# Two attention decodes in one kernel: five rows of B's output weights loaded in sixteen small pieces, to a tile of their own

## The chip, the cores and the metric

The kernel runs on one core of one Trainium2 chip. The metric is the device time of one execution in microseconds (us). Before the change the median of three runs is 255.6 us (255.55 to 255.86).

## The reference, cut to what matters

The program computes two independent attention steps, A and B, for one query position each, and puts their outputs side by side. Each has 32 query heads and 16 key/value heads of 128 elements (two query heads share one key/value head), a model width of 576, and a cache of 8192 positions. A looks only at the last 2048 of them, B at all.

```
q = (x @ wq)                       # 576 -> 32 heads x 128
scores = q . k * 128 ** -0.5       # A: last 2048 positions, B: all 8192
o = softmax(scores) . v
out = o.reshape(1, 32 * 128) @ wo  # 4096 -> 576, for A and for B
return concatenate([a, b], axis=-1)
```

All inputs are bf16. The caches that are read are the bulk: 2 MB of K and 2 MB of V for each of B's 16 heads, 512 KB each for A's. `wq` and `wo` have 4.7 MB for each problem.

## The kernel before, in words

**Instructions and their waits.** The kernel is written as five lists of instructions, one for each engine's queue. `op` (L41) puts a compute instruction on a list, `load` (L47) a DMA. Each names the instructions or loads that it needs; `emit` (L53) turns these names into waits on semaphores, in the order of the list, so an instruction that waits holds up what stands behind it on its queue. A load adds 16 to its semaphore when it has landed.

**The ring.** Nearly all that is loaded goes through one large buffer, `ring` (L112), 86 x 1024 bf16 elements in each of 128 partitions. `place` (L165) gives a load the next stretch of it, starting over at the end, and makes the load wait for the last users of whatever stood there before. It also cycles through 24 semaphores. All loads of weights and caches are issued by SyncE (the queue named SPq), one after the other: first A's and B's `wq`, then the units, then `wo`.

**Units and slabs.** A unit is the K or the V of one head of one problem (L195 to L199): 64 units, 32 of 2 MB for B and 32 of 512 KB for A, of which the V units come some units behind their K. Partition p holds a run of consecutive positions of the cache, so each load has an outer dimension of 128 partitions and one long run in each (16 KB for B, 4 KB for A). A unit is worked on in slabs of 2048 positions, four for B and one for A, so 80 slabs for K and 80 for V. `units` is walked at L457, where `place` is called for each (L464).

**Work on a slab.** TensorE transposes the 16 tiles of a K slab (`st_T`, L310), ScalarE and VectorE copy them out (L328, L331), TensorE multiplies with the query (`st_S`, L342). When the five slabs of a head are done, a shared maximum, the exponential and a transpose of the probabilities follow, and nine slabs behind K, TensorE multiplies them with V (`st_V`, L426). The heads' outputs are turned and collected in `oT` (L453).

**The end.** After the last head the sums are divided out, and `oP` (L527) holds the outputs as 32 columns for each problem: partition p of column k stands for row 32 * p + k of the output weights. So `wo` is loaded with 32 of its rows in each partition (1152 bytes a row), in the pieces that `NWO` lists (L28): two of 16 rows for A, and 8, 8, 6, 4, 3, 2 and 1 for B (L471 to L478). The rows of a piece are consecutive in each partition. For each piece, TensorE runs two matmuls a row (one for each half of the 576 columns), each 1 x 288 wide, accumulated over the 32 rows (L533 to L543, named F0.c for A and F1.c for B). A piece's matmuls wait for that piece alone. Behind A's two pieces and behind B's last piece, ScalarE and VectorE each copy out one half (L547, L550), and SyncE stores the result (L551), a load in reverse with an outer dimension of 2.

Of the kernel before, what the change touches and what calls it, by code (L numbers as in the profile page):

```python
# [4 lines left out]
BF16 = mybir.dt.bfloat16  # L5
# [6 lines left out]
HQ = 32  # L12
G = 16
DH = 128
DM = 576
# [4 lines left out]
SLAB = 2048  # L20
NI = SK // SLAB + 1
IA = NI - 1
RING = 86 * 1024
NSEM = 24
NKT = 3
LAG = 9
QP = 32 * NI
NWO = [[16, 16], [8, 8, 6, 4, 3, 2, 1]]  # L28


class Prog:
# [9 lines left out]
    def op(self, eng, fn, deps=(), name=None):  # L41
        self.ops[eng].append((fn, tuple(deps), name, None))
        if name is not None:
            assert name not in self.where, name
            self.where[name] = (eng, len(self.ops[eng]) - 1)

    def load(self, eng, fn, sem, value, deps=(), name=None):  # L47
        self.ops[eng].append((fn, tuple(deps), None, sem))
        if name is not None:
            assert name not in self.dma, name  # L50
            self.dma[name] = (sem, value)
# [54 lines left out]
def bass_concat_heads__sliding_block_cached__gqa_block_cached__decode_kernel(nc, A_x, A_k_cache, A_v_cache, A_wq, A_wo,  # L106
                         B_x, B_k_cache, B_v_cache, B_wq, B_wo, out):
    xs, ks, vs = [A_x, B_x], [A_k_cache, B_k_cache], [A_v_cache, B_v_cache]
    wqs, wos = [A_wq, B_wq], [A_wo, B_wo]


    ring = nc.alloc_sbuf_tensor("ring", [128, RING], BF16)  # L112
    ktb = nc.alloc_sbuf_tensor("ktb", [128, NKT, SLAB], BF16)
# [23 lines left out]
    oq = nc.alloc_sbuf_tensor("oq", [128, 2, HQ], BF16)  # L137
    oP = nc.alloc_sbuf_tensor("oP", [128, 2, HQ], BF16)
    warm = nc.alloc_sbuf_tensor("warm", [128, 8], F32)
    outsb = nc.alloc_sbuf_tensor("outsb", [128, 288], BF16)  # L140

    tb = [nc.alloc_psum_tensor("tb%d" % b, [128, 512], F32) for b in range(3)]
# [13 lines left out]
    op, load = pg.op, pg.load  # L156
    s_x = nc.alloc_semaphore("s_x")
    s_ld = [nc.alloc_semaphore("s_ld%d" % i) for i in range(NSEM)]
    s_out = nc.alloc_semaphore("s_out")


# [3 lines left out]
    def place(size, uses, issue, name):  # L165
        if at[0] + size > RING:
            at[0] = 0
        lo, hi = at[0], at[0] + size
        at[0] = hi
        deps = []  # L170
        for r in list(live):
            if r[0] < hi and lo < r[1]:
                deps += r[2]
                live.remove(r)
        n = nload[0]
        nload[0] += 1
        if n >= NSEM:
            deps += uses_of[n - NSEM]
        uses_of.append(list(uses))
        live.append((lo, hi, list(uses)))  # L180
        t = ring[:, lo:hi]
        load("sp", lambda e: issue(e, t), s_ld[n % NSEM], 16 * (n // NSEM + 1), deps=deps, name=name)
        return t
# [4 lines left out]
    NS = G * NI  # L188
# [6 lines left out]
    units = []  # L195
# [6 lines left out]
    def slab_ap(kind, s):  # L202
# [8 lines left out]
       deps=["id0"], name="ident")  # L211
# [9 lines left out]
    for c in range(2):  # L221
        op("dve", lambda e, c=c: e.tensor_reduce(par[:, c:c + 1], view(identf, 128, c, [[2, 64]]), AX.X, ALU.add),
           deps=["identf"], name="par%d" % c)
# [7 lines left out]
    for P in range(2):  # L231
# [6 lines left out]
            s_x, 64, name="x%d" % P)  # L238
# [17 lines left out]
    for P in range(2):  # L256
        op("dve", lambda e, P=P: e.tensor_copy(  # L257
            xrep[:, P, 0:4, :], xsb[:, P, 0:4].unsqueeze(2).to_broadcast([128, 4, 32])),
            deps=["x%d" % P], name="xr%da" % P)
        for c in range(2):  # L260
            op("dve", lambda e, P=P, c=c: e.tensor_scalar(  # L261
                xrep[:, P, 4 + c, :], xsb[:, P, 4:5].to_broadcast([128, 32]), par[:, c:c + 1], None, ALU.mult),
                deps=["x%d" % P, "par%d" % c], name="xr%d%s" % (P, "bc"[c]))

    def q_proj(P):
        banks = tb[0:2] if P == 0 else sb
        for k in (0, 1, 2, 3, 5):
            for n in range(8):
                def mm(e, k=k, n=n):
                    j = n % 4  # L270
                    if k < 4:
                        x, w = xrep[:, P, k, :], wq_at[P, k // 2][:, (k % 2) * HQ * DH + n * 512:][:, 0:512]
                    else:
                        x, w = xrep[:, P, 4 + n // 4, :], wq_at[P, 2][:, (n % 4) * 512:(n % 4 + 1) * 512]
                    return e.matmul(banks[n // 4][32 * j:32 * j + 32, :], lhsT=x, rhs=w,  # L275
                                    start=(k == 0), stop=(k == 5))
                op("pe", mm, deps=["wq%d.%d" % (P, k // 2), "xr%da" % P, "xr%db" % P, "xr%dc" % P],
                   name="qmm%d.%d.%d" % (P, k, n))
# [54 lines left out]
    def st_S(k):  # L333
        g, i = divmod(k, NI)
        deps = ["E%d" % (2 * k), "E%d" % (2 * k + 1)]
        if i == 0:
            deps += q_ready
            deps += ["exp%d" % (g - 2), "max%d" % (g - 2)] if g >= 2 else ["qe1.0", "qe1.1"]

        def mm(e):  # L340
            for j in range(4):
                ins = e.matmul(sb[g % 2][32 * j:32 * j + 32, :], lhsT=qz[:, g, 32 * i:32 * i + 32],  # L342
                               rhs=ktb[:, k % NKT, j * 512:(j + 1) * 512],
                               start=(i == 0), stop=(i == IA))
            return ins
        op("pe", mm, deps=deps, name="S%d" % k)
# [65 lines left out]
    def st_V(v):  # L412
        g, i = divmod(v, NI)
        ab = 1 if i == IA else 0
        deps = ["V.%d" % v, "PE%d" % g]
        if i == 0:
            deps += ["xo%d" % (g - 1)] if g >= 1 else ["vb0"]

        def mm(e):
            src = slab_ap("V", v)  # L420
            for pair in range(2):
                for j in range(4):
                    t0 = 4 * j + 2 * pair
                    c0 = (j * NI + i) * 8 + 4 * pair
                    lhsT = pts[:, g % 2, c0:c0 + 4]
                    ins = e.matmul(vb[32 * j:32 * j + 4, 256 * ab:256 * ab + 256], lhsT=lhsT,  # L426
                                   rhs=src[:, t0:t0 + 2, :],
                                   start=(i in (0, IA) and pair == 0),
                                   stop=(i in (IA - 1, IA) and pair == 1))
            return ins  # L430
        op("pe", mm, deps=deps, name="V%d" % v)
# [22 lines left out]
               deps=["OT%d" % g], name="or%s%d" % (nm, g))  # L454


    for u in units:  # L457
        kind, g, small = u
        P = 0 if small else 1
        src = (ks if kind == "K" else vs)[P][0, g, SK - W_A if small else 0:SK, :].rearrange(  # L460
            "(p t) d -> p (t d)", p=128)
        slabs = [g * NI + IA] if small else [g * NI + i for i in range(IA)]
        nm = "u%s%d%d" % u
        where[u] = place((W_A if small else SK) // 128 * DH,  # L464
                         [("T%d.1" if kind == "K" else "V%d") % slabs[-1]],
                         lambda e, t, src=src: e.dma_start(t, src), nm)
        for i in slabs:
            pg.dma[("K%d" if kind == "K" else "V.%d") % i] = pg.dma[nm]


    wo_at = {}  # L471
    for P in range(2):
        k0 = 0
        for c, kk in enumerate(NWO[P]):
            src = wos[P].rearrange("(p k) n -> p (k n)", k=HQ)[:, k0 * DM:(k0 + kk) * DM]
            wo_at[P, c] = place(kk * DM, ["F%d.%d" % (P, c)], lambda e, t, src=src: e.dma_start(t, src),  # L476
                                "wo%d.%d" % (P, c))
            k0 += kk  # L478
# [4 lines left out]
    for k in range(slots + 2):  # L483
# [33 lines left out]
       deps=["lsel", "nb%d" % (G - 1), "mrA%d" % (G - 1), "mrB%d" % (G - 1)], name="L")  # L517
# [12 lines left out]
    fb = tb[0]  # L530
    for P in range(2):
        k0 = 0
        for c, kk in enumerate(NWO[P]):  # L533
            def mm(e, P=P, c=c, k0=k0, kk=kk):
                for k in range(kk):
                    for n in range(2):
                        r = 32 * (2 * P + n)
                        ins = e.matmul(fb[r:r + 1, 0:288], lhsT=oP[:, 1 - P, k0 + k:k0 + k + 1],  # L538
                                       rhs=wo_at[P, c][:, k * DM + 288 * n:k * DM + 288 * n + 288],
                                       start=(k0 + k == 0), stop=(k0 + k == HQ - 1))  # L540
                return ins
            op("pe", mm, deps=["wo%d.%d" % (P, c), "oP", "E%d" % (2 * NS - 1), "E%d" % (2 * NS - 2),
                               "E%d" % (2 * NS - 3)], name="F%d.%d" % (P, c))  # L543
            k0 += kk
        last = "F%d.%d" % (P, len(NWO[P]) - 1)
        r = 64 * P
        op("act", lambda e, r=r: e.activation(outsb[r:r + 1, :], fb[r:r + 1, 0:288], ACT.Copy),  # L547
           deps=[last], name="f%d.0" % P)
        r = 64 * P + 32
        op("dve", lambda e, r=r: e.tensor_copy(outsb[r:r + 1, :], fb[r:r + 1, 0:288]), deps=[last], name="f%d.1" % P)  # L550
        load("sp", lambda e, P=P: e.dma_start(  # L551
            out[0, 0:1, P * DM:(P + 1) * DM].rearrange("o (n c) -> (o n) c", n=2),
            bass.AP(tensor=outsb, offset=64 * P * 288, ap=[[32 * 288, 2], [1, 288]])),
            s_out, 16 * (P + 1), deps=["f%d.0" % P, "f%d.1" % P], name="out%d" % P)
# [32 lines left out]
```

## Time and profile before

| | |
|---|---|
| median of three runs | 255.6 us |
| the profiled execution: its own time | 255.6 us |
| its span, first to last instruction | 253.8 us |
| mean granted TensorE clock | 0.926 |
| TensorE matmuls, busy | 181.7 us (72%) |
| TensorE weight loads, busy | 122.8 us (48%) |
| ScalarE, busy | 104.8 us (41%) |
| VectorE, busy | 84.9 us (33%) |
| moved by DMA | 103.15 MB, mean 406 GB/s |

A span runs from the first to the last instruction of the profiled execution; what an execution takes beyond it is start and end. Busy times of the engines lie beside each other and are no sum. Lines are named by engine: PE is TensorE, PEld its weight loads, DVE is VectorE, ACT is ScalarE, POOL is GpSimd, SP is SyncE, and a q behind a name means the queue that issues (SPq issues the loads). A tile on the left of `<-` is written, those on its right are read. A DMA share of 1.00 means that all sixteen transfer queues of the core were occupied throughout a stretch. The chain of work that ended last is followed back from the last instruction, at each step to what released it.

### The profile page before, as it was taken

What the parts mean: (1) busy time and instruction counts of PE and PEld (TensorE: products, weight loads), DVE (VectorE), ACT (ScalarE), POOL (GpSimd) and SP (SyncE); (2) the same over time, 40 slices, a digit from 0 to 9 for tenths busy, and PEclk for the clock granted to TensorE, in tenths of its full rate; (3) what the DMA queues carried; (4) which work ended last, traced back from release to release, by engine and by line L of the source; (5) the groups of instructions that cost most, each with busy time, mean ns of one, the idle gap of its engine ahead of it and who ended that gap; (6) DMA issues with size and microseconds to landing.
All of it is one profiled execution on the core that took longest, in us unless ns stands there. A gap on an engine that the chain in (4) does not pass through costs nothing.

```text
span 253.8 us, 5887 instructions
## 1 busy us (share of the span) xinstructions
PE 181.7 (72%) x2659; PEld 122.8 (48%) x2659; DVE 84.9 (33%) x256; ACT 104.8 (41%) x134; POOL 3.8 (1%) x12
## 2 busy tenths in 40 slices
PE   0002989495979595979398959795979298965764
PEld 0001367373756374657276737473657275733331
DVE  1001156252526161535152615351635053533000
ACT  2000067462547372547045735472547055730000
POOL 5000000000000000000000000000000000000000
PEclk9999999999899998899769998997999679998589
DMA  7999999999999999999999999999999999999981
GB/s 261 401 366 409 425 422 440 414 427 422 428 414 424 418 438 405 429 424 426 414 428 422 425 412 435 420 425 421 413 422 431 422 415 425 426 432 417 417 366 76
DMA packets 11985, 103.15 MB, mean 406 GB/s; under 512 B 1844, under 2 KB 1976, under 8 KB 6840
## 3 DMA queue, kind: packets, MB, share of 16 engines
q1 hardware_dynamic: 11384, 102.77, 97.0%
q8 instruction: 21, 0.34, 0.6%
q10 hardware_dynamic: 576, 0.00, 0.1%
q14 instruction: 4, 0.03, 0.0%
HBM read 102.76 MB, written 0.00 MB: 405 GB/s over the span
## 4 chain that ended last, share of the span: by engine, by line
DMA 90%; PE 5%; SPq 2%; issue 1%; ACT 0%; DVE 0%; ACTq 0%
DMA ring<-in_B_k_cache_dram 71%; DMA ring<-in_B_wo_dram 11%; DMA xsb<-in_B_x_dram 8%; PE tb L310 2%; SPq L476 2%; PE tb L275 2%; PE sb L342 0%; ACT L219 0%; PE tb L538 0%; ACTq L233 0%; PE vb L426 0%; DVE outsb L550 0%; DVE xrep L257 0%; DVE xrep L261 0%; ACTq L236 0%
## 5 line engine op out<-in xcount | busy, mean ns | idle before, releaser
L310 PE MATMUL tb<-ident,ring 128*128 128x128 bf16 x1280 | 92.4, 230 | 34.7 <-DMA ring<-in_B_k_cache_dram 34.5
L328 ACT ACTIVATE ktb<-tb 128x1024 bf16<-128x1024 bf16 x80 | 81.6, 1021 | 82.8 <-PE tb L310 82.8
L310 PEld LDWEIGHTS tb<-ident,ring 128*128 128x128 bf16 x1280 | 78.1, 103 | 54.1 <-DMA ring<-in_B_k_cache_dram 38.7
L331 DVE COPY ktb<-tb 128x1024 bf16<-128x1024 bf16 x80 | 55.3, 692 | 113.1 <-PE tb L310 112.2
L426 PE MATMUL vb<-ring,pts 128*4 128x256 bf16 x640 | 35.2, 283 | 0.0
L342 PE MATMUL sb<-ktb,qz 128*32 128x512 bf16 x320 | 33.3, 406 | 0.0
L275 PE MATMUL tb<-ring,xrep 128*32 128x512 bf16 x40 | 4.5, 631 | 23.9 <-DVE xrep L257 23.9
L426 PEld LDWEIGHTS vb<-ring,pts 128*4 128x4 bf16 x640 | 15.1, 85 | 9.4 <-issue 4.1
L538 PE MATMUL tb<-ring,oP 128*1 128x288 bf16 x128 | 12.2, 366 | 5.4 <-DMA ring<-in_B_wo_dram 3.3
L275 PEld LDWEIGHTS tb<-ring,xrep 128*32 128x32 bf16 x40 | 1.6, 142 | 25.9 <-issue 25.9
L390 ACT ACTIVATE psb<-sb,nb 128x512 bf16<-128x512 f32 x16 | 11.0, 687 | 6.4 <-DVE nb L384 6.4
L437 ACT ACTIVATE xo<-vb 128x512 f32<-128x512 f32 x16 | 9.6, 597 | 7.9 <-PE vb L426 7.9
L342 PEld LDWEIGHTS sb<-ktb,qz 128*32 128x32 bf16 x320 | 8.3, 93 | 7.5 <-issue 1.4
L538 PEld LDWEIGHTS tb<-ring,oP 128*1 128x1 bf16 x128 | 6.0, 103 | 11.5 <-DMA ring<-in_B_wo_dram 5.2
L445 PE MATMUL ob<-identf,xo 128*128 128x128 f32 x64 | 10.5, 287 | 1.4 <-ACT xo L437 1.4
L279 ACT ACTIVATE qsb<-tb 128x512 bf16<-128x512 f32 x1 | 0.6, 597 | 25.8 <-PE tb L275 25.8
L352 DVE TENSOR_REDUCE mx<-sb 128x1 f32<-128x512 f32 x16 | 10.9, 682 | 0.8 <-PE sb L342 0.8
L445 PEld LDWEIGHTS ob<-identf,xo 128*128 128x128 f32 x64 | 6.7, 140 | 5.2 <-issue 3.2
L547 ACT ACTIVATE outsb<-tb 1x288 bf16<-1x288 f32 x2 | 0.8, 400 | 20.2 <-PE tb L538 20.2
L400 PE MATMUL mb<-ident,psb 128*128 128x128 bf16 x64 | 6.4, 222 | 0.7 <-ACT psb L390 0.7
L257 DVE COPY xrep<-xsb 128x128 bf16<-128x128 bf16 x2 | 0.4, 224 | 18.5 <-DMA xsb<-in_B_x_dram 18.5
L550 DVE CAST outsb<-tb 1x288 bf16<-1x288 f32 x2 | 0.9, 458 | 16.8 <-PE tb L538 16.8
(51 smaller groups left out, 64.4 us busy)
## 6 DMA issues: line engine op xcount, KB each, us to landing
ring<-in_B_k_cache_dram SPq DMA_DIRECT2D x16, 2048.0 KB, 36.0
ring<-in_B_v_cache_dram SPq DMA_DIRECT2D x16, 2048.0 KB, 33.7
ring<-in_A_k_cache_dram SPq DMA_DIRECT2D x16, 512.0 KB, 33.6
ring<-in_A_v_cache_dram SPq DMA_DIRECT2D x16, 512.0 KB, 33.4
ring<-in_A_wo_dram SPq DMA_DIRECT2D x2, 2304.0 KB, 36.7
ring<-in_A_wq_dram SPq DMA_DIRECT2D x2, 2048.0 KB, 9.8
ring<-in_B_wq_dram SPq DMA_DIRECT2D x2, 2048.0 KB, 20.8
ring<-in_B_wo_dram SPq DMA_DIRECT2D x2, 1152.0 KB, 35.0
```

What stands on the lines that cost most here:

```text
L275: return e.matmul(banks[n // 4][32 * j:32 * j + 32, :], lhsT=x, rhs=w, start=(k == 0), stop=(k == 5))
L310: ins = e.matmul(tbh[n % 3][:, t * 128:(t + 1) * 128], lhsT=src[:, 8 * half + t, :], rhs=ident[:, :], start=True, stop=True, is_transpose= ...
L328: op("act", lambda e, n=n, dst=dst: e.activation(dst, tbh[n % 3], ACT.Copy), deps=deps, name="E%d" % n)
L331: op("dve", lambda e, n=n, dst=dst: e.tensor_copy(dst, tbh[n % 3]), deps=deps, name="E%d" % n)
L342: ins = e.matmul(sb[g % 2][32 * j:32 * j + 32, :], lhsT=qz[:, g, 32 * i:32 * i + 32], rhs=ktb[:, k % NKT, j * 512:(j + 1) * 512], start=(i ...
L352: op("dve", lambda e: e.tensor_reduce(mx[:, 0:1], sb[g % 2][:, :], AX.X, ALU.max), deps=deps, name="max%d" % g)
L390: op("act", lambda e: e.activation(psb[:, g % 2, :], sb[g % 2][:, :], ACT.Exp, bias=nb[:, g % 2:g % 2 + 1], scale=SCALE, accum_out=rsall[: ...
L400: ins = e.matmul(mbh[:, 512 + t * 128:512 + (t + 1) * 128], lhsT=psb[:, g % 2, t * 128:(t + 1) * 128], rhs=ident[:, :], start=True, stop=T ...
L426: ins = e.matmul(vb[32 * j:32 * j + 4, 256 * ab:256 * ab + 256], lhsT=lhsT, rhs=src[:, t0:t0 + 2, :], start=(i in (0, IA) and pair == 0), ...
L437: op("act", lambda e: e.activation(xo[:, :], vb[:, :], ACT.Copy), deps=deps, name="xo%d" % g)
L445: ins = e.matmul(ob[:, c * 128:(c + 1) * 128], lhsT=xo[:, c * 128:(c + 1) * 128], rhs=identf[:, :], start=True, stop=True, is_transpose=True)
L538: ins = e.matmul(fb[r:r + 1, 0:288], lhsT=oP[:, 1 - P, k0 + k:k0 + k + 1], rhs=wo_at[P, c][:, k * DM + 288 * n:k * DM + 288 * n + 288], st ...
```

## The change

Of the 32 rows of B's `wo` in each partition, the first five are no longer loaded into the ring behind the units. They go to a tile of their own, `woe` (5 x 576 elements in each partition). It is filled by sixteen loads of eight partitions each, 5760 bytes in each partition, 46 KB a load. Load n covers the partitions p0, p0 + 4, ..., p0 + 28 with p0 = 32 * (n // 4) + n % 4. SyncE issues one of them ahead of every third unit, from unit 6 to unit 51. They need no slot of the ring and wait for nothing. They share one semaphore, of which the full value of 256 is waited for.

The other 27 rows stay in seven pieces, now of 8, 7, 5, 3, 2, 1 and 1 rows. On TensorE the ten matmuls of the five rows stand ahead of B's first piece, behind A's. The ring becomes 2 x 1024 elements smaller.

```diff
-RING = 86 * 1024
+RING = 84 * 1024
...
-NWO = [[16, 16], [8, 8, 6, 4, 3, 2, 1]]
+NWO = [[16, 16], [8, 7, 5, 3, 2, 1, 1]]
+NE = 5
...
+    woe = nc.alloc_sbuf_tensor("woe", [128, NE * DM], BF16)
...
+    s_e = nc.alloc_semaphore("s_e")
...
+    def dma_woe(n):
+        p0 = 32 * (n // 4) + n % 4
+        w = wos[1]
+        src = bass.AP(tensor=w.tensor, offset=w.offset + p0 * HQ * DM, ap=[[4 * HQ * DM, 8], [1, NE * DM]])
+        dst = bass.AP(tensor=woe, offset=p0 * NE * DM, ap=[[4 * NE * DM, 8], [1, NE * DM]])
+        load("sp", lambda e: e.dma_start(dst, src), s_e, 256, name="woe" if n == 15 else None)
+
+    for nu, u in enumerate(units):
+        if nu % 3 == 0 and 6 <= nu < 54:
+            dma_woe(nu // 3 - 2)
...
-        k0 = 0
+        k0 = NE * P
...
+        pieces = [(wo_at[P, c], kk, "wo%d.%d" % (P, c)) for c, kk in enumerate(NWO[P])]
+        if P == 1:
+            pieces.insert(0, (woe, NE, "woe"))
+        for c, (wt, kk, ld) in enumerate(pieces):
+            def mm(e, P=P, wt=wt, k0=k0, kk=kk):
...
-                                       rhs=wo_at[P, c][:, k * DM + 288 * n:k * DM + 288 * n + 288],
+                                       rhs=wt[:, k * DM + 288 * n:k * DM + 288 * n + 288],
```

More of the change, by code (lines that the diff above doesn't have):

```diff
@@ L454, in st_or @@
                deps=["OT%d" % g], name="or%s%d" % (nm, g))
-    for u in units:
+    def dma_woe(n):
[7 more added lines that the diff above has]
+            dma_woe(nu // 3 - 2)
         kind, g, small = u
@@ L532, in bass_concat_heads__sliding_block_cached__gqa_block_cached__decode_kernel @@
         k0 = 0
-        for c, kk in enumerate(NWO[P]):
-            def mm(e, P=P, c=c, k0=k0, kk=kk):
+        pieces = [(wo_at[P, c], kk, "wo%d.%d" % (P, c)) for c, kk in enumerate(NWO[P])]
[3 more added lines that the diff above has]
+            def mm(e, P=P, wt=wt, k0=k0, kk=kk):
                 for k in range(kk):
@@ L538, in mm @@
                         ins = e.matmul(fb[r:r + 1, 0:288], lhsT=oP[:, 1 - P, k0 + k:k0 + k + 1],
-                                       rhs=wo_at[P, c][:, k * DM + 288 * n:k * DM + 288 * n + 288],
+                                       rhs=wt[:, k * DM + 288 * n:k * DM + 288 * n + 288],
                                        start=(k0 + k == 0), stop=(k0 + k == HQ - 1))
                 return ins
-            op("pe", mm, deps=["wo%d.%d" % (P, c), "oP", "E%d" % (2 * NS - 1), "E%d" % (2 * NS - 2),
-                               "E%d" % (2 * NS - 3)], name="F%d.%d" % (P, c))
+            op("pe", mm, deps=[ld, "oP", "E%d" % (2 * NS - 1), "E%d" % (2 * NS - 2),
+                               "E%d" % (2 * NS - 3)], name="F" + ld[2:])
             k0 += kk
```

## The prediction

> **What bounds the kernel now.** I read the chain of work that ended last first, because it names what the end waits for.
>
> ```profile
> DMA 90%; PE 5%; SPq 2%; issue 1%; ACT 0%; DVE 0%; ACTq 0%
> ...
> 221.75 28.89 DMA ring<-in_B_wo_dram
> 250.64 0.04 issue
> 250.68 0.67 PE tb L538 x6
> 251.35 0.02 issue
> 251.38 0.46 DVE outsb L550
> ```
>
> Nine tenths of the chain are transfers, and it ends in B's output weights: after the last landing only a few small matmuls, one eviction and the store are left. So the end moves with the last landing. Next, the table by stretches (length, busy time of PE, PEld, DVE, ACT and POOL, granted clock, DMA share, GB/s):
>
> ```profile
> 200.00:225.00 25.00, 21.68 (x326) 15.13 (x326) 10.71 (x33) 12.65 (x16) 0.00 (x0) 0.88 1.02 425
> ...
> 241.00:247.45 6.45, 4.31 (x58) 2.36 (x52) 0.45 (x1) 0.40 (x1) 0.00 (x0) 0.82 0.90 368
> 247.45:249.00 1.55, 0.96 (x14) 0.51 (x16) 0.00 (x0) 0.00 (x0) 0.00 (x0) 1.00 0.51 200
> 249.00:251.00 2.00, 1.45 (x18) 0.47 (x18) 0.00 (x0) 0.00 (x0) 0.00 (x0) 1.00 0.23 84
> ```
>
> The sixteen transfer queues are full until about 241 us; then the share falls to a half and a quarter while the end still waits for data. They do not finish together. The trace records sixteen completions of every 128-partition load; those of the very last one come at 246.01, .16, .28, .52, .59, .72, .82 (seven queues), 248.25 (one), 249.14, .48, .49, .55 (four) and 250.82, .97, 251.00, 251.00 (four). Their mean is 248.4, so 2.6 us at most could be had by perfect sharing. Where the lateness comes from stands in the page's table of queues:
>
> ```profile
> q1 hardware_dynamic: 11384, 102.77, 97.0%
> q8 instruction: 21, 0.34, 0.6%
> ```
>
> There are 21 instruction transfers of 16 KB, 1.02 to 1.11 us each, and their durations repeat with a period of eight. After the first (start 33.7 us) one completion of the next load is 1.34 us behind the other fifteen (39.42 against 38.08). Eight queues taking turns give five with three and three with two; the 21st starts only at 249.03, when its queue is about done. That is the four and four. The queue at 248.25 fits none: it fell behind by steps (0.7 us near 71 us, 0.4 near 170, 0.6 near 190). I call it the straggler, and "light" all eight queues without instruction transfers, it among them.
>
> Last, the wait list of SyncE's queue and the load issues: B's weights land 26 to 35 us after their issue, so the queues hold some 26 us of work even at the end and no queue runs dry.
>
> **The change, part by part.**
>
> *Bytes taken out of the sixteen queues.* A queue carries eight partitions of each large load. The records give, for a partition's packet of 1, 2, 3, 4, 6 and 8 rows, 51, 93, 135, 178, 262 and 347 ns, back to back. Before: 347+347+262+178+135+93+51 = 1413 ns. After, with 7 rows between 6 and 8 (304) and 5 between 4 and 6 (220): 347+304+220+135+93+51+51 = 1201. Saved: 212 ns by eight partitions = 1.70 us on every queue.
>
> *Sixteen loads of eight partitions added.* A load of outer dimension 2, the store of an output, is in the records exactly two packets of 576 B; so I take outer dimension 8 as eight packets on eight queues. Each of the eight gets, for each of the sixteen loads, one packet of 5760 B (220 ns, as above), a 4 B completion packet (9 ns) and a gap (5 ns): 16 x 234 = 3.74 us. Which eight? The trace identifies two: the two packets of the first store ran at 245.85 and 246.41, right where light queues ended their last load (completions of 246.0 to 246.6; the last four were then still over 4 us from done). I take the other six to be light as well. Light queues then change by 3.74-1.70 = +2.04 us, the others by -1.70. The bounds: eight queues that are all light (-1.70 for the late ones), or some late queue among them (+2.04 for it).
>
> [...]
>
> *What an added packet costs under load.* Every queue moves 16,384 B in 611 ns at best and 614 ns in the median, so nothing here has slack. Eight of the sixteen loads go to partitions 64 to 127. If such a packet shares anything with a packet of another queue, it lies between 220 ns (shares nothing) and 440 (takes turns with an equal), and it takes between 0 and 220 ns from the other queue. No row shows two queues on the same partitions; the nearest is the 614 ns median in a stream where all sixteen run at once and hardly slow each other. I take 220 and keep both ends.
>
> [...]
>
> *SyncE's queue.* Sixteen issues more, between the units. An issue that is not held up takes 0.33 to 0.43 us and the two stores, of two rows, 0.49 and 0.62, so 16 x 0.62 = 10 us over some 190 us. Behind each stand the next unit's wait for its slot and its issue. They are covered: SyncE spends up to 6.5 us inside a single issue, and the units land 33 to 36 us after it. Without that cover it would cost the 10 us.
>
> *The smaller ring.* Followed through the code of `place`, every unit and every weight piece waits for the same instructions as before, so this costs nothing. The tightest is the first B piece: its slot is freed at 208.83, it is issued at 208.88, and its landing begins at 237.60, which leaves the cover of 28 us that the rest has too.
>
> *TensorE.* Ten matmuls move ahead of the first B piece and wait for all sixteen loads, of which the last stands beside a unit that is issued at 155.7 and lands by 190.4, some 50 us earlier than needed.
>
> ```profile
> 239.89 4.27 PE L538 MATMUL tb<-ring,oP 128*1 128x288 bf16 x48 [1.52 <-DMA ring<-in_A_wo_dram]
> ...
> 245.45 1.14 PE L538 MATMUL tb<-ring,oP 128*1 128x288 bf16 x16 [1.28 <-DMA ring<-in_B_wo_dram]
> ```
>
> At 4.27/48 = 0.089 us they take 0.89 us, inside the 1.28 us in which PE waits here. Without that gap they would cost 0.9 us. The last piece stays one row, so what follows the last landing stays.
>
> *Sum.* Completions of the last load: late queues 251.00-1.70 = 249.30, ordinary light ones 246.82+2.04 = 248.86, straggler 248.25+2.04 = 250.29. The straggler is last: 0.71 us earlier than 251.00. The profiled execution took 255.6 us for a span of 253.8, which is also the median of the runs, so 255.6-0.7 = **254.9 us**.
>
> **Rivals.**
>
> *No straggler.* Its steps look like chance; without them the last is a late queue at 249.30, and the time is 255.6-1.7 = 253.9. Against it: the profile that I have shows one.
>
> *Packets that collide (slower).* Place: the eight loads to partitions 64 to 127. Price: 440+14 = 454 ns for each on a light queue, so 8 x 234 + 8 x 454 - 1.70 = +3.80; and 8 x 220 - 1.70 = +0.06 for the queue collided with. The straggler ends at 252.05, and the time is 255.6+1.05 = 256.7. It decides from the point where the straggler gains more than 251.00-248.25 = 2.75 us, that is (2.75+1.70)/16 = 278 ns for each added packet with its completion, 44 over my 234. For it: full queues. Against it: the stream's packets, hardly slower than the best.
>
> *Collision without a straggler, or spreading over all sixteen.* In the first, late queues end at 251.06 and light ones at 250.62: 255.7. In the second each queue gets eight packets, 8 x 0.234 - 1.70 = +0.17: 255.8. No change either way.
>
> *A late queue among the eight.* It ends at 251.00+2.04: 257.6. Against it: both queues that the trace identifies are light.
>
> **How the numbers follow.** Forecast 254.9, chance 0.30; no straggler 253.9, 0.15; no change 255.7 to 255.8, 0.20; colliding packets 256.7, 0.27; a late queue among the eight 257.6, 0.08. A measurement of this kernel can tell about 0.2% from no change, 0.5 us; so faster 0.45, same 0.20, slower 0.35. The range 253.8 to 256.7 leaves out the last case. Cases of both signs hold most of the chance; the likeliest one's own range is 253.9 (a straggler that gains nothing on the rest) to 255.3 (half the way to the breaking point, 22 ns more for each packet).
>
> **What would show it.** In the profile after: the last load's sixteen completions. Right: four at 249.3, the light ones near 248 to 249, and a DMA share near 0.9 until 247. Colliding: added packets of some 400 ns, the late four still at 251. Spread: sixteen queues that all end some 0.2 us later than now. SyncE: units still land over 25 us after issue. What would make the prediction wrong above all is a cost per added packet over 278 ns.

## The result, and the profile after

The changed kernel takes 259.36 us in the median of six runs (258.63 to 260.17), against 255.60 before: 1.0147 times the time, 95% interval 1.0118 to 1.0176. The profiled execution took 258.63 us for a span of 256.8, 3.0 us more than before. The forecast was 254.9 with a range up to 256.7.

The chain of work that ended last still ends in B's output weights, and what follows the last landing is as short as before:

```profile
229.57 24.44 DMA ring<-in_B_wo_dram
254.01 0.04 issue
254.05 0.30 PE tb L554 x2
254.38 0.46 DVE outsb L566
```

The last landing came at 254.01 where it had been at 251.00. The table by stretches (columns as in the prediction, the last two are DMA share and GB/s) shows where it was lost. First three stretches of the kernel before, then those of the changed kernel:

```profile
125.00:150.00 25.00, 20.95 (x304) 14.73 (x304) 9.71 (x28) 12.65 (x16) 0.00 (x0) 0.89 1.01 423
150.00:175.00 25.00, 20.43 (x304) 14.31 (x304) 9.72 (x28) 12.65 (x16) 0.00 (x0) 0.93 1.01 421
175.00:200.00 25.00, 20.21 (x304) 14.08 (x304) 9.72 (x28) 12.65 (x16) 0.00 (x0) 0.91 1.01 424
```

```profile
50.00:75.00 25.00, 20.39 (x304) 14.03 (x304) 9.64 (x26) 12.66 (x16) 0.00 (x0) 0.93 1.01 422
75.00:100.00 25.00, 20.40 (x304) 14.27 (x304) 9.71 (x28) 12.65 (x16) 0.00 (x0) 0.91 1.01 423
...
125.00:150.00 25.00, 21.13 (x294) 14.98 (x295) 9.46 (x28) 12.53 (x16) 0.00 (x0) 0.86 1.01 408
150.00:175.00 25.00, 20.85 (x312) 14.35 (x314) 10.05 (x29) 12.78 (x17) 0.00 (x0) 0.93 1.02 406
175.00:200.00 25.00, 18.28 (x240) 12.63 (x236) 7.84 (x24) 9.11 (x11) 0.00 (x0) 0.80 1.01 408
200.00:225.00 25.00, 20.38 (x308) 14.19 (x312) 9.79 (x29) 12.74 (x17) 0.00 (x0) 0.93 1.01 423
...
241.00:247.45 6.45, 6.25 (x74) 3.19 (x72) 0.04 (x1) 0.04 (x1) 0.00 (x0) 0.62 0.99 409
247.45:249.00 1.55, 1.12 (x18) 0.58 (x16) 0.41 (x1) 0.36 (x1) 0.00 (x0) 1.00 0.87 361
249.00:251.00 2.00, 1.02 (x14) 0.52 (x14) 0.00 (x0) 0.00 (x0) 0.00 (x0) 1.00 0.79 306
```

Two things are to be read here. From 125 to 200 us the queues move 406 to 408 GB/s in place of 421 to 424, while their share stays at 1.01 to 1.02: they are as busy as ever and slower. 75 us at 15 GB/s less are 1.1 MB, some 2.7 us of the core's transfers. The first eight added loads land between 49 and 115 us, where the rate is untouched; the last eight land between 125 and 196 us. And the end is no evener than before: the sixteen completions of the last load come at 247.40 and .48 (two queues), 250.63 to 252.71 (twelve), 253.69 and 254.01. Their mean is 251.33, 2.90 us later than the 248.43 of before; the prediction had 0.17.

The transfer records between 125 and 195 us tell who pays. The added packets of 5760 bytes took 241 ns in the mean, hardly more than the 224 ns of the earlier ones. But all other packets got longer: those of 16 KB from 618 ns (before) to 638 in the mean, one in ten over 705 (before: 620), and those of 4 KB from 162 to 173. Over the 1349 and 1450 packets of these two sizes that is 27 and 16 us, 43 us of queue time in all; the sixteen queues together ended 16 x 2.73 = 44 us later than without a loss (the 2.73 is worked out in the table further down). So the longer packets of the others account for the lost rate.

### The profile page after: what moved, and what is told of

Read it like the earlier page. It is cut to its first block, busy times and chain, and to the rows that moved or that the text cites. A ratio compares the mean times of both kernels' runs of the same rounds, so it can differ in the third digit from the quotient of the medians.

```text
span 256.8 us, 5903 instructions
## 1 busy us (share of the span) xinstructions
PE 185.5 (72%) x2659; PEld 125.1 (49%) x2659; DVE 85.2 (33%) x256; ACT 104.8 (41%) x134; POOL 3.8 (1%) x12
## 4 chain that ended last, share of the span: by engine, by line
DMA 72%; SPq 14%; PE 12%; issue 0%; DVE 0%
DMA ring<-in_B_k_cache_dram 63%; DMA ring<-in_B_wo_dram 10%; PE tb L313 8%; SPq L479 6%; SPq L466 4%; SPq L489 3%; PE sb L345 2%; PE vb L429 1%; SPq L250 1%; PE mb L403 0%; SPq L253 0%; PE mb L382 0%; PE mb L361 0%; DVE outsb L566 0%; PE tb L554 0%
## 5 line engine op out<-in xcount | busy, mean ns | idle before, releaser
L313 PE MATMUL tb<-ident,ring 128*128 128x128 bf16 x1280 | 95.4, 234 | 35.7 <-DMA ring<-in_B_k_cache_dram 35.4
L313 PEld LDWEIGHTS tb<-ident,ring 128*128 128x128 bf16 x1280 | 80.7, 105 | 55.8 <-DMA ring<-in_B_k_cache_dram 39.8
L429 PE MATMUL vb<-ring,pts 128*4 128x256 bf16 x640 | 36.2, 290 | 0.0
L345 PE MATMUL sb<-ktb,qz 128*32 128x512 bf16 x320 | 34.8, 426 | 0.0
L278 PE MATMUL tb<-ring,xrep 128*32 128x512 bf16 x40 | 3.9, 563 | 24.3 <-DVE xrep L260 24.3
L554 PE MATMUL tb<-ring,oP 128*1 128x288 bf16 x118 | 11.1, 341 | 3.1 <-DMA ring<-in_B_wo_dram 2.4
L554 PEld LDWEIGHTS tb<-ring,oP 128*1 128x1 bf16 x118 | 5.3, 96 | 8.8 <-DMA ring<-in_B_wo_dram 4.5
L361 PE MATMUL mb<-identf,mx 128*1 128x128 f32 x32 | 6.4, 280 | 0.6 <-DVE mx L355 0.6
```

Source lines behind the costliest of these rows:

```text
L313: ins = e.matmul(tbh[n % 3][:, t * 128:(t + 1) * 128], lhsT=src[:, 8 * half + t, :], rhs=ident[:, :], start=True, stop=True, is_transpose= ...
```

## The experiments

The theory that I started from (D, later M) was the prediction's rival of colliding packets: a packet would be expensive when its queue writes partitions that another queue fills. Its rivals were that loads on eight of sixteen queues (the trace records eight completions for each) hurt whatever their destination (F), and that the loss has nothing to do with the added loads (R).

**One half of the loads alone.** The tile's other half is zeroed early, and its rows are left out of the result.

```diff
-        if nu % 3 == 0 and 6 <= nu < 54:
+        if nu % 3 == 0 and 6 <= nu < 30:     (e1; e2: 30 <= nu < 54)
```

> Only the first eight of the sixteen added loads are issued, those to partitions 0 to 63; the five rows of partitions 64 to 127 are left out and stand as zeros. Theory D (destination: packets to partitions 64 to 127 collide with the queues that fill these partitions, packets to 0 to 63 don't): the late queues are 1.7 us earlier than before and the light ones 8 x 0.234 - 1.7 = 0.2 us later, so 253.9 us, at most 254.9 with a straggler. Theory F (form: any load on eight of sixteen queues disturbs the stream, wherever it goes): half of the excess of 4.5 us that the changed kernel shows over the forecast, so about 256.1. Theory R (the rest: the split pieces, the order on TensorE, the smaller ring): about 259.

> Only the last eight of the sixteen added loads are issued, those to partitions 64 to 127; the five rows of partitions 0 to 63 are left out and stand as zeros. Theory D: nearly the whole loss stays, less what the other eight loads take on the light queues (up to 1.9 us), so 257.5 to 259.4, and the moved GB/s fall in the same stretch (some 125 to 195 us) as in the changed kernel. Theory F: about 256.1, as with the first eight. Theory R: about 259.

Measured: 255.14 us for the first half (253.94 to 255.64; ratio 0.9969, 0.9953 to 0.9985) and 258.03 for the second (1.0089, 1.0072 to 1.0105). The same number of packets of the same size on the same number of queues: the second half takes 2.9 us more than the first. The stretches of the first half's kernel and of the second half's, in this order:

```profile
75.00:100.00 25.00, 20.32 (x304) 14.18 (x304) 9.71 (x28) 12.67 (x16) 0.00 (x0) 0.93 1.01 422
...
150.00:175.00 25.00, 20.44 (x304) 14.10 (x304) 9.81 (x28) 12.66 (x16) 0.00 (x0) 0.93 1.01 423
```

```profile
75.00:100.00 25.00, 18.97 (x306) 13.30 (x307) 9.71 (x28) 12.65 (x16) 0.00 (x0) 1.00 1.01 423
...
150.00:175.00 25.00, 19.67 (x302) 13.60 (x300) 9.23 (x29) 12.26 (x16) 0.00 (x0) 0.93 1.01 407
```

Of the two halves only the loads to partitions 64 to 127 lower the rate, to 407 GB/s at worst (of the first half's kernel no stretch from 25 to 241 us is under 421). F is out. The first half's time is a partial miss, though: up to 255.64 where D expected at most 254.9. That is taken up below.

**No small loads.** One load of 128 partitions ahead of unit 30 fills the same tile.

```diff
...
+        if nu == 30:
+            load("sp", lambda e: e.dma_start(
+                woe[:, :], wos[1].rearrange("(p k) n -> p (k n)", k=HQ)[:, 0:NE * DM]), s_e, 16, name="woe")
```

> The five rows come in one load of 128 partitions ahead of unit 30, in place of the sixteen; tile, pieces, order on TensorE and ring stay as in the changed kernel. Theories D and F: the time of the kernel before, 255.6 +- 0.4. Theory R: about 259.

Measured: 255.72 us, ratio 1.0002 (0.9993 to 1.0011). Tile, pieces, order on TensorE and ring cost nothing, as predicted; R is out. The sixteen issues are not in this kernel; the next one has them.

**The same bytes to the lower partitions.** The sources stay; the rows of partitions 64 to 127 land behind those of 0 to 63.

```diff
-        dst = bass.AP(tensor=woe, offset=p0 * NE * DM, ap=[[4 * NE * DM, 8], [1, NE * DM]])
+        dst = bass.AP(tensor=woe, offset=(p0 % 64) * 2 * NE * DM + (n // 8) * NE * DM, ap=[[8 * NE * DM, 8], [1, NE * DM]])
...
+    op("pe", lambda e: e.matmul(mb[0:64, 128:128 + NE], lhsT=perm[:, 64:128], rhs=oq[:, 0, 0:NE],
...
```

> The same sixteen loads of the same bytes, but the five rows of partitions 64 to 127 land in partitions 0 to 63, behind their own five; the ten matmuls of five rows become twenty of 64 partitions, and one small matmul and two copies bring the outputs that belong to these rows to the lower partitions. The ring has 82 x 1024 elements. Theory D: no collisions, so what the prediction summed: 254 to 255. Theory F: as the changed kernel, 259 to 260. Theory R: about 259.

Measured: 256.61 us (255.44 to 257.49), ratio 1.0033 (1.0017 to 1.0050). From 259.36 the other destination takes back 2.75 us, with the same sources and the same sixteen issues, and the rate of this kernel is whole again:

```profile
125.00:150.00 25.00, 21.02 (x315) 14.21 (x313) 9.93 (x29) 12.65 (x17) 0.00 (x0) 0.93 1.01 423
150.00:175.00 25.00, 20.28 (x304) 14.15 (x304) 9.71 (x28) 12.64 (x16) 0.00 (x0) 0.93 1.01 423
175.00:200.00 25.00, 21.11 (x296) 14.75 (x296) 9.80 (x28) 12.64 (x16) 0.00 (x0) 0.86 1.01 422
```

Yet D's 254 to 255 was missed by 1.6 us. So there is a second loss, without any loss of rate: the work is shared badly.

**Upper half, or mismatch?** Lower partitions alone, eight next to each other in place of eight that are four apart; then all rows in eight loads of sixteen partitions, with the same number of packets on every queue (the trace records sixteen completions for each).

```diff
-        p0 = 32 * (n // 4) + n % 4
+        p0 = 8 * n      (e5; steps of one partition)
+        p0 = n          (e8; sixteen partitions in steps of eight)
...
```

> As e1_first_half (partitions 0 to 63 alone, the five rows of the others left out as zeros), but load n covers the eight consecutive partitions 8n to 8n + 7 in place of eight that are four apart. Theory M (mismatch: a packet costs the others whenever its queue writes partitions that another queue fills): like e2_second_half, 257 to 259. Theory U (it is the upper half of the partitions as such): like e1_first_half, 254 to 255.6.

> All five rows in eight loads of sixteen partitions, eight apart (n, n + 8, ..., n + 120), so that all sixteen queues get the same number of packets and nothing is shifted between queues; nearly every packet goes to partitions that another queue fills. Theory M: 128 packets at 0.6 us of queue time are 77 us, 4.8 us on each of the sixteen: 259 to 261. If shifting work between queues is what hurts: as before, 255.4 to 256.

Measured: 258.03 us for the first (1.0093, 1.0078 to 1.0107), the very time of the second half, and 259.72 for the second (1.0164, 1.0146 to 1.0182). The stretches of the first and of the second, where their added loads land:

```profile
50.00:75.00 25.00, 21.99 (x304) 15.17 (x304) 9.65 (x26) 12.64 (x16) 0.00 (x0) 0.86 1.01 407
75.00:100.00 25.00, 19.68 (x281) 13.85 (x282) 9.12 (x27) 11.47 (x15) 0.00 (x0) 0.86 1.02 405
```

```profile
50.00:75.00 25.00, 21.23 (x304) 14.77 (x304) 9.65 (x26) 12.64 (x16) 0.00 (x0) 0.88 1.01 408
75.00:100.00 25.00, 21.56 (x304) 14.86 (x304) 9.81 (x28) 12.64 (x16) 0.00 (x0) 0.86 1.02 397
```

So the rate falls without the upper partitions (405 GB/s), and with no work shifted between queues (397). Steps of four partitions in the lower half keep the rate (421 to 424 GB/s), steps of one or eight do not. A mismatch of queue and partition (M) fits all of these; but the trace does not say which of the sixteen queues carried a packet, so it is inferred and not shown. These two kernels also read the rows of the weights in another order; that the destination decides rests on the kernel with the lower destinations, which keeps the sources of the changed one.

The runs show what such loads cost: the lowest stretch of 25 us is at 397 to 408 GB/s in each of these kernels, in place of 422; what in the hardware makes them cost it is not measured here.

**Half the cost.** The last four of the sixteen loads alone.

> Only the last four of the sixteen loads are issued (partitions 96 to 127); the five rows of the other partitions are left out as zeros. If the price is one for each packet (some 0.6 us of queue time, 44 us in all for 64 packets in the changed kernel and some 39 in e2_second_half), half of the price of e2_second_half: its sixteen completions of the last load have a mean some 1.2 us above 247.2 and the time is about 256 (255.3 to 256.8). If the first collisions set off a lasting disorder, near 258.

Measured: 255.85 us (255.41 to 256.20), ratio 1.0008 (0.9999 to 1.0017), and 408 and 409 GB/s from 150 to 200 us with 423 before and after. Its stretches:

```profile
125.00:150.00 25.00, 20.33 (x304) 14.20 (x304) 9.71 (x28) 12.64 (x16) 0.00 (x0) 0.93 1.01 423
150.00:175.00 25.00, 21.46 (x304) 14.86 (x304) 9.80 (x28) 12.65 (x16) 0.00 (x0) 0.87 1.01 408
175.00:200.00 25.00, 21.24 (x295) 14.88 (x295) 9.62 (x28) 12.56 (x16) 0.00 (x0) 0.86 1.01 409
200.00:225.00 25.00, 19.50 (x276) 13.48 (x274) 8.88 (x27) 11.01 (x15) 0.00 (x0) 0.86 1.01 423
```

The cost goes with the packets and leaves no lasting disorder (423 GB/s again from 200 us). The price of one follows from the mean of the last load's sixteen completions, compared with what packets of 234 ns and the saved rows would give. How many packets mismatch is an estimate from the first half, which kept the rate: if the partitions of a load go to its queues in order (an assumption, which the trace does not show), queue i of the eight wrote partitions 4i to 4i+3 and 32+4i to 35+4i there, and these are taken to be its own. In the two mixed kernels a few packets would then fall on their queue's own partitions, 8 of 64 and (with the upper half laid out alike) 16 of 128.

| kernel | packets that mismatch (estimate) | mean | without collisions | queue time lost, for each packet |
|---|---|---|---|---|
| changed kernel | 64 | 251.33 | 248.60 | 2.73 x 16 / 64 = 0.68 us |
| second half alone | 64 | 250.08 | 247.67 | 0.60 us |
| first half, mixed | 56 | 250.83 | 247.67 | 0.90 us |
| last four alone | 32 | 248.64 | 247.20 | 0.72 us |
| sixteen, mixed | 112 | 252.05 | 248.60 | 0.49 us |
| first half alone | 0 | 247.53 | 247.67 | none |
| lower destinations | 0 | 248.17 | 248.60 | none |

The two kernels counted without a mismatch lie 0.14 and 0.43 us below the sum, so with 64 packets a price is known to about 0.1 us, with 32 to about 0.2.

**The second loss.** The completions of the first half's kernel tell of it: 244.55 and 244.58; 246.06 to 246.85 (five); 247.76 and .77; 248.21; 249.12 to 249.42 (six). A queue with neither queue 8's instruction transfers nor added packets should be 1.70 us earlier than 246.0 to 246.8 was, and two are. Had the eight queues of the added loads been the eight light ones, there would be none. So two light queues were left out, and by this count two of the eight carry instruction transfers (theory L).

Why the runs spread is in the instruction transfers, too. Their eight durations are a signature: in the profile before, they run 1016, 1074, 1068, 1069, 1105, 1100, 1094, 1026 ns and start again; in the profile after, 1074, 1069, 1059, 1107, 1109, 1095, 1016, 1018. That looks like the same turn, begun at its second queue. So which queues get a third transfer would differ from one execution to the next. Before the change that would make no difference (its runs lie within 255.42 to 255.86), because by the same count four queues have three at either start; now it would decide whether a queue with added packets has two or three.

To try this, two rows went to four queues alone, by theory L without instruction transfers (sixteen loads of outer dimension 4, with two runs of 2304 bytes in each partition, to partitions 0 to 15 and 32 to 47; the outputs that belong to them are brought there by four small matmuls):

```diff
-NE = 5
+NE = 2
...
+        dst = bass.AP(tensor=woe, offset=(2 * p0 + h) * 2 * NE * DM,
+                      ap=[[16 * NE * DM, 4], [NE * DM, 2], [1, NE * DM]])
...
```

> Full computation. Two rows (in place of five) are moved, in sixteen loads of outer dimension 4 to partitions 0 to 15 and 32 to 47, two runs of 2304 bytes in each: four queues get 32 packets each. Theory L (of the eight queues of the added loads two also carry instruction transfers, which e1_first_half's completions suggest; the lowest four carry none; and no packet collides): late queues end 0.67 us earlier, at 250.3, the four at 249 to 249.3: 254.8 to 255.1, and four queues of the last load's sixteen, without packets of either kind, are 0.67 us earlier than before. If an instruction queue is among the four: it ends near 252, 256.5.

Measured: 255.07 us (254.97 to 255.19), ratio 0.9976 (0.9966 to 0.9986), faster than both kernels. Four queues end at 245.42 to 246.32, 0.5 to 0.6 us earlier than the light ones of before (246.01 to 246.82). So four of the eight light queues have no added packets, and all four with added packets are light. The chain of this kernel ends with the last landing at 250.51, half a microsecond earlier than before:

```profile
225.00 25.51 DMA ring<-in_B_wo_dram
250.55 0.31 PE tb L574 x2
250.88 0.47 DVE outsb L586
```

Then the same with three rows (29 in the pieces), and the eight queues of the lower destinations with two rows:

> As e6_four_queues, but three rows in place of two: the four queues get 32 x 135 + 16 x 14 = 4.54 us and lose 1.01, so +3.53; the late ones -1.01, to 250.0. If the straggler (248.25 before) is not one of the four, they end at 249.5 to 250.4 and the time is 254.7 to 255.0, a little under that of two rows. If it is one of them, it ends at 251.8: 256.4.

> As e4_low_destinations (eight queues, all destinations in partitions 0 to 63), but two rows in place of five. Each of the eight queues gets 16 x (93 + 14) ns less 0.67 = +1.04 us, the others -0.67. Theory L (two of the eight also carry two instruction transfers each, which puts them at 249.5 before): these two end at 250.5, the late four at 250.3, so 255.1 (255.0 to 255.4), and the runs agree better than those of e4_low_destinations, since nothing but these sets the end. Without instruction queues among the eight: 254.9.

Three rows on four queues: 255.95 us (255.78 to 256.73), ratio 1.0014 (1.0006 to 1.0023). One queue ends at 251.26, all others by 249.88: the straggler is one of the four, as in the expectation's second case, 0.45 us cheaper. It came back in every profile where it could be told, so it was not chance.

What makes it late can be read in the trace. Besides the 21 instruction transfers of queue 8 there are four smaller ones, of 8 KB and some 0.32 us each:

```profile
q14 instruction: 4, 0.03, 0.0%
```

In the profile before they start at 70.61, 86.58, 169.65 and 225.34. At the first, one light queue leaves the others (at most 0.62 us behind the first completion of their load) and stands at 1.32; at the third it goes from 1.31 to 2.29, and it ends at 2.25: that is the straggler. The kernel with one load repeats it (to 1.34 at 69.8, from 1.38 to 2.32 at 172.5), and with three rows the last queue goes from 4.51 to 5.48 at 170.5. The second and the fourth transfer put one light queue each back by some 0.65 us, which stays hidden among the light ones. The completions do not name their queues; this is read from the order and the times, not tried by an experiment.

Two rows on eight queues: 256.12 us (254.87 to 256.94), ratio 1.0012 (0.9997 to 1.0026). My expectation named only the case of two instruction transfers, 255.1; with three, the same sum gives 251.0 + 1.04 = 252.0 and 256.6, and the runs lie between just below the one and just above the other. The runs of two rows on four queues (254.97 to 255.19) have no such spread.

Last, the first half with an outer dimension of 6:

```diff
-        src = bass.AP(tensor=w.tensor, offset=w.offset + p0 * HQ * DM, ap=[[4 * HQ * DM, 8], [1, NE * DM]])
+        src = bass.AP(tensor=w.tensor, offset=w.offset + p0 * HQ * DM, ap=[[4 * HQ * DM, 6], [1, NE * DM]])
```

> As e1_first_half, but with an outer dimension of 6 in place of 8: the last two of the eight partitions of each load are left out as well (zeros, like partitions 64 to 127). In e1_first_half the runs spread from 253.9 to 255.6. Theory L (two of the eight queues take turns in the instruction transfers; the turn starts elsewhere in each execution, so they sometimes have three and then set the end), with the two being the last of the eight: without them nothing but the late queues sets the end, and all runs lie within 253.6 to 254.3. If the two are among the first six, the spread stays.

Measured: 254.00 us (ratio 0.9950, 0.9934 to 0.9967); four runs lie between 253.69 and 254.04, two at 255.08 and 255.22. So the expectation held for four runs of six. Three queues, not two, ended at 244.1 to 244.6, which says, by the count used for the first half, that one of the six still carries instruction transfers. The other of the two would then be among the two of the eight that are left out, and none among the four of outer dimension 4.

## Why the prediction was wrong, point by point

- **What bounds the kernel, and where the lateness comes from: right.** The chain ends with the last landing of B's weights in the profiles of both kernels, of the lower destinations and of the four queues, and the completions put the lateness down to the instruction transfers: in the profile before, one of them is 1.34 us behind the other fifteen after the first transfer (39.42 against 38.08). The four transfers of queue 14 were left out of account.
- **Bytes taken out, 1.70 us: right.** The latest queues of the first half's kernel ended at 249.1 to 249.4, 1.6 to 1.7 us earlier than their like before (250.8 to 251.0).
- **Packets and queues of an added load: right in number.** The trace records eight completions for each (and one increment at its issue), four with an outer dimension of 4, sixteen with 16.
- **"I take the other six to be light as well": wrong.** This is the first step that failed. By the completions of the first half's kernel, two of the eight carry instruction transfers. With the rate whole, in the kernel with the lower destinations, the time is still above that of before: 256.61 us.
- **"I take 220 and keep both ends": wrong, and the upper end was too low.** This is the step that failed worst. Between a packet that shares nothing and one that takes turns I allowed 0.44 us, both sides together, and chose the lower end because the stream's packets hardly slow each other (611 ns at best, 614 in the median); but if in the stream each queue keeps to its own partitions, as the experiments suggest and no row shows, that row could not show a collision. The completions give 0.49 to 0.90 us for each packet counted as mismatching, 0.68 in the changed kernel, and not where I looked for it: the packet itself stays near 240 ns, the other packets get longer (those of 16 KB from 618 to 638 ns). Over 64 packets that is 2.7 us on each queue. The two steps add up: from the forecast of 254.9 to the 256.61 of the kernel with the lower destinations, and from there 2.75 us to 259.36.
- **The rivals.** Colliding packets gave 256.7, and a late queue among the eight 257.6, as alternatives. Both were true at once, and the first dearer than its price, so the time lies beyond both. That the eight loads to partitions 64 to 127 are the place of it, and that the other packet loses at most 220 ns, no row of before shows. In the changed kernel the rate fell where these eight land (406 to 408 GB/s), but with eight partitions next to each other it fell in the lower half alone as well (405 to 409).
- **SyncE's queue, the ring, TensorE: right.** The one load in place of sixteen gives the time of before. The sixteen issues to the lower partitions left the rate whole (421 to 424 GB/s from 25 to 241 us). An added issue took 0.65 to 10.1 us, since most were held up like the others; the caches' loads still landed 31 to 34 us after theirs in the median, where it had been 33 to 36. (Before, the longest single issue took 7.86 us, not 6.5; the cover is the larger for it.)
- **"Its steps look like chance": wrong.** The straggler stays, by the three rows it is among the four queues of outer dimension 4, and its steps near 71 and 170 us come with queue 14's transfers of 70.61 and 169.65. The second step is some 0.95 us and not 0.4. The one near 190 us is none, as the completions are best read: there another queue goes from 1.69 to 3.21 with the instruction transfer that starts at 191.61, past the straggler, which stays at 2.3.

What stays open: whether it is the mismatch of queue and partition that costs, why such a packet costs the others two to four times its own length (0.49 to 0.90 us against 0.24), and which of the other queues pay. The rise from 254.0 to 255.1 in two of six runs of the last experiment is some six tenths of the 1.87 us that a third instruction transfer on one of the six queues would give by the sum, so that assignment is likely, not shown.

## What to carry to other kernels

When transfers bound a kernel, look at how evenly its queues end before moving bytes between them, and identify the late queues by an experiment that marks them; two out of sixteen taken wrongly turned the gain around. In these kernels a small load of eight partitions beside a saturated stream left the rate whole (421 to 424 GB/s) when it went to the lower half in steps of four partitions; to the upper half, or in steps of one or eight, it slowed the stream (397 to 408 GB/s in the lowest stretch of each kernel). A row that shows no conflict proves nothing for a case in which the conflict could not have occurred.

## What the runs showed of the hardware

- For each packet of 5760 bytes that is counted as mismatching (an estimate, see the table), 0.49 to 0.90 us of queue time were lost, while the queues' share still reads 1.01 to 1.02: here the share does not show the loss, the GB/s do (422 to 397 at worst).
- The instruction transfers of queue 8, 21 of 16 KB in each of the two profiles before and after, seem to go over eight queues in turn, by the period of eight in their durations (1016 to 1107 ns before) and by the completions: before, four are 3.0 us and four 4.5 us behind the seven first in the mean, taken to be two and three transfers, so some 1.5 us for each. The turn seems to begin at another queue in another execution.
- With each of the four instruction transfers of queue 14, of 8 KB and some 0.32 us, one queue fell back by some 0.65 to 0.98 us, by the order and the times of the completions; two of these steps, near 71 and 170 us, are the straggler's.
- The trace records four completions for each load with outer dimension 4, and by the last load's completions their four queues carried none of queue 8's transfers: moving two rows there made the kernel 0.24% faster (255.07 us, interval of the ratio 0.9966 to 0.9986).
